# The last 448 tokens of unit 1: a short convolution on GpSimd instead of one TensorE group, with the products in one lasting tile

## The chip, the cores and the metric

The kernel runs on one core of one Trainium2 chip. The metric is the time of one execution on the device in microseconds. Three runs of the kernel before gave 765.89, 766.1 and 766.1 us; their median is 766.1.

Five engines work side by side, each in the order of its own instruction list: TensorE (PE in the profile; PEld is its loading of weights), VectorE (DVE), ScalarE (ACT), GpSimd (POOL) and SyncE (SP, used here to issue DMAs). They wait for each other through semaphores.

## What is computed

Eight sequences of 4096 tokens with 192 features pass through a causal convolution of seven taps. The features are split into eight heads of 24; each head has its own seven taps, normalised by a softmax. A feed-forward layer with a gate follows.

```python
# convolution: x (8, 4096, 192), weight (8, 7)
w = exp(weight - max) / sum                       # over the seven taps
out[b, s, h, g] = sum_k w[h, k] * x_pad[b, s + k, h, g]   # six zeros ahead of token 0
# feed-forward, on 32768 tokens, d_ff = 1536
gate = np.maximum(x @ w_gate, 0.0)
val = x @ w_val
return (gate * val @ w_out)
```

## The kernel before

**Layout.** Sequences are taken in pairs: sequence b and sequence b + 4 (called streams, st = 0 and 1). A unit is 1024 tokens of both streams, so there are 4 x 4096 / 1024 = 16 units. In the convolved input xc of a unit, the 192 features are three chunks of 64; the first 64 partitions hold stream 0, the other 64 stream 1, and tokens run along the free axis.

**A unit on TensorE.** For each window w of 512 tokens, gate_val (line 528) multiplies xc with w_gate and w_val, twelve blocks of 128 columns (line 541); ScalarE applies the Relu (line 552) and VectorE multiplies gate and value into hT (line 553). Then project (line 636) multiplies hT with w_out in eight half passes (line 570), ScalarE copies the results out of PSUM (line 596; the last of a unit is shared with VectorE) and SyncE issues their stores. So TensorE runs, unit by unit: gate_val of window 0, gate_val of window 1, project.

**The convolution of the next unit** is made beside this. GpSimd loads x with a cast to f16 (lane_load, line 203) with 64 tokens ahead of each piece (the halo), copies it into the order for the transpose (lane_turn, line 465), and SyncE issues nine DMA transposes, which give x_r with features on the partitions (line 469). The first 576 tokens of a unit (LDVE) are then made by ScalarE and VectorE: ScalarE the first tap (lane_first, line 501), VectorE the other six, three chunks each, as one multiply-and-add into acc and, for the last tap, into xc (lane_rest, line 515). VectorE has no other work in that stretch, which lies beside project. The other 448 tokens (LPOOL) are made from products per tap, written into prods by ScalarE and VectorE (line 485 and 487; the five of VectorE are listed in VECTOR, among them tap 1 of chunk 2 as the last), which GpSimd adds up in the next unit (add, line 491): six adds over 3 x 448 elements, the last one into xc. The piece of 448 tokens that is loaded and multiplied with unit v is that of unit v + 1, so that GpSimd has a whole unit for its adds.

**The start.** Unit 0 has nothing ahead of it, so both its windows are convolved on TensorE (conv_dense, line 377), with matrices (bands) that hold the taps along a diagonal. Unit 1's first 576 tokens are made as usual during unit 0. Its last 448 tokens have no unit before them to be multiplied in: they are loaded as a third group of four blocks of 112 tokens (load_x(2)), convolved by eight matmuls between unit 0's gate_val and its project (conv, line 411), cast out of PSUM by five ScalarE instructions into y (conv_out, line 430), and turned by four DMA transposes into xc of unit 1 (conv_turn, line 453).

**Order.** Nothing is rescheduled: each engine's instructions stand in the order in which the program issues them (manual_schedule), and semaphores follow from the tiles that they read and write. GpSimd's order at the start is: copies of weights to the second 64 partitions (pool_halves), w_out's load (Wo), more copies, the load of unit 1, a copy of the taps to the second 64 partitions (tap), the load of the third group, the copies of unit 1 for its transposes; then, in the loop, the load of unit 2, which is held until ScalarE's first lane_first instruction. The 448-token products of each unit take a fresh prods tile from a pool with one buffer. In unit 1 two products (FOR_POOL) are made by GpSimd.

Of the kernel before, what the change touches and what calls it, by code (L numbers as in the profile page):

```python
# [8 lines left out]
FP = mybir.dt.float32  # L9
# [6 lines left out]
def kernel(  # L16
# [38 lines left out]
    FIRST = WIN - DSUB * (GSUB - 1)  # L55
    GROUPS = [(0, [0] + [FIRST + DSUB * j for j in range(GSUB - 1)])]
    GROUPS += [(0, [WIN + DSUB * j for j in range(GSUB)])]
    GROUPS += [(0, list(range(UNIT + LDVE, 2 * UNIT, SUB)))]

    ctx.enter_context(tc.manual_schedule())  # L60
    const = ctx.enter_context(tc.tile_pool(name="const", bufs=1))
# [1 line left out]
    epool = ctx.enter_context(tc.tile_pool(name="epool", bufs=1))  # L63
    rpool = ctx.enter_context(tc.tile_pool(name="rpool", bufs=2))
    apool = ctx.enter_context(tc.tile_pool(name="apool", bufs=1))
    ypool = ctx.enter_context(tc.tile_pool(name="ypool", bufs=1))
    xcpool = ctx.enter_context(tc.tile_pool(name="xcpool", bufs=3))
    hpool = ctx.enter_context(tc.tile_pool(name="hpool", bufs=2))
    gpool = ctx.enter_context(tc.tile_pool(name="gpool", bufs=3))
# [4 lines left out]
    def load_x(g):  # L74


        bp, toks = GROUPS[g]
        n, rows, step = len(toks), SUB if g < 2 else 128, toks[1] - toks[0]
        xt = xts[g] = xpool.tile([128, GSUB, 2, D], F16, name="x_h")
        for st in range(2):  # L80
            src = bass.AP(
                tensor=x.tensor,
                offset=x.offset + ((bp + NB * st) * S + toks[0] - PAD) * D,
                ap=[[D, rows], [step * D, n], [1, D]],
            )
            nc.gpsimd.dma_start(out=xt[0:rows, 0:n, st, :], in_=src)
            yield

    def load_rest(steps):
        for _ in steps:  # L90
            pass
# [87 lines left out]
    def pool_halves(s):  # L179
        both_halves(nc.gpsimd.tensor_copy, s, Wg)  # L180
        both_halves(nc.gpsimd.tensor_copy, s, Wv)
# [160 lines left out]
    def band(h):  # L342
        return bands[h]
# [2 lines left out]

    PLACE = {0: (0, 0, 0), 1: (0, 0, 1), 3: (0, 1, 0), 4: (0, 1, 1)}
    PLACE |= {6: (1, 0, 0), 7: (1, 0, 1), 2: (1, 1, 0), 5: (1, 1, 1)}  # L350

    def conv_dense(g, c, ps, bank):


# [44 lines left out]
        conv_dense(1, 2, one, 0)  # L399
        nc.vector.tensor_copy(out=xc[0][:, 2, WIN : 2 * WIN], in_=one[:, 0, :])  # L400

    def conv(g):


        xt = xts[g]
        n = len(GROUPS[g][1])
        rows = SUB + PAD
        W = 2 * n * G
        wide = [psum.tile([128, 2, 512], FP, name="ps") for _ in range(2)]
        for h, (t, bank, slot) in PLACE.items():  # L410
            nc.tensor.matmul(  # L411
                out=wide[t][0:SUB, bank, W * slot : W * (slot + 1)],
                lhsT=band(h),
                rhs=xt[0:rows, 0:n, :, G * h : G * (h + 1)],
                start=True,
                stop=True,
                skip_group_check=True,
            )
        return wide

    def conv_out(g, wide):
        bp, toks = GROUPS[g]
        n = len(toks)
        W = 2 * n * G
        y = ypool.tile([128, GSUB, NCH, 2, 64], F16, name="y")

        def move(copy, t, bank, i0, step_in, c, r0, step_out, width):
            src = wide[t][0:SUB, bank, 0 : 2 * W]
            dst = y[0:SUB, 0:n, 0, :, 0:1]
            copy(  # L430
                out=bass.AP(
                    tensor=dst.tensor,
                    offset=dst.offset + 128 * c + r0,
                    ap=[dst.ap[0], [step_out, 2], [NCH * 128, n], [64, 2], [1, width]],
                ),
                in_=bass.AP(
                    tensor=src.tensor,
                    offset=src.offset + i0,
                    ap=[src.ap[0], [W + step_in, 2], [2 * G, n], [G, 2], [1, width]],
                ),  # L440
            )

        move(nc.scalar.copy, 0, 0, 0, 0, 0, 0, G, G)
        move(nc.scalar.copy, 0, 1, 0, 0, 1, 8, G, G)
        move(nc.scalar.copy, 1, 0, 0, 0, 2, 16, G, G)
        move(nc.scalar.copy, 1, 1, 0, 8, 0, 48, 2 * 128 - 48, 16)
        move(nc.scalar.copy, 1, 1, 16, -16, 1, 0, 56, 8)
        return y

    def conv_turn(g, y):  # L450
        for jj, t in enumerate(GROUPS[g][1]):
            u, k = t // UNIT, min(SUB, UNIT - t % UNIT)
            nc.sync.dma_start_transpose(
                out=xc[u][:, :, t % UNIT : t % UNIT + k],
                in_=y[0:k, jj].rearrange("p c s r -> p (c s r)"),
            )

    def lane_turn(v):
        xe = xes.pop(v)
        xp = epool.tile([128, TILES, NCH, 2, 64], F16, name="x_p")  # L460
        xr = rpool.tile([128, NCH, 128 * TILES], F16, name="x_r")
        xrs[v] = xr
        for j0, n, _ in pieces(v):
            for st in range(2):
                nc.gpsimd.tensor_copy(  # L465
                    out=xp[:, j0 : j0 + n, :, st, :], in_=xe[:, j0 : j0 + n, st, :, :]
                )
            for j in range(j0, j0 + n):
                nc.sync.dma_start_transpose(
                    out=xr[:, :, 128 * j : 128 * j + 128],  # L470
                    in_=xp[:, j].rearrange("p c s r -> p (c s r)"),
                )
            yield

    def shifted(v, c, k, lane):
        o = HALO - KW + 1 + k
# [34 lines left out]
    def lane_rest(v):  # L511
        acc = accs.pop(v)
        for k in range(1, KW):
            for c in range(NCH):
                nc.vector.scalar_tensor_tensor(  # L515
                    out=xc[v][:, c, 0:LDVE] if k == KW - 1 else acc[:, c, :],
                    in0=shifted(v, c, k, 0),
                    scalar=tap[:, c, k : k + 1],
                    in1=acc[:, c, :],
                    op0=ALU.mult,  # L520
                    op1=ALU.add,
                )
        if v + 1 < NUNIT:
            prods[v] = apool.tile([128, KW, NCH, LPOOL], FP, name="prods")
            for c, k in VECTOR:
                product(nc.vector, v, c, k)

# [108 lines left out]
    def project(u, hs, work):  # L636
        bp, w0 = u * UNIT // S, u * UNIT % S // WIN
        at, done = {}, {}
        order = [(0, 0), (1, 0), (0, 1), (2, 0), (1, 1), (3, 0), (2, 1), (3, 1)]
        if u == NUNIT - 1:  # L640
            order = [(0, 0), (1, 0), (0, 1), (1, 1), (2, 2), (3, 2)]
        for i, turn in order:
            h, st = hs[i // 2], i % 2
            row0 = (bp + NB * st) * S + WIN * (w0 + i // 2)
            if turn == 2:
                whole_half(h, st, row0, i == 3)
                continue
            if turn == 0:
                at[i] = slots()
            else:  # L650
                for c, k in work[i]:
                    product(nc.scalar, u + 1, c, k)
            done[i] = half_pass(h, st, at[i][1], turn, done.get(i))
            if turn:
                evict(at[i][0], row0, i == 3)
# [3 lines left out]
    both_halves(nc.vector.tensor_copy, 1, Wg)  # L659
    both_halves(nc.vector.tensor_copy, 1, Wv)  # L660
    pool_halves(4)
    nc.gpsimd.dma_start(out=Wo[:], in_=moe_w_out.rearrange("(c p) d -> p c d", p=128))
    pool_halves(5)
    load_rest(lane_load(1))
    nc.gpsimd.tensor_copy(out=tap[64:128], in_=tap[0:64])
    load_rest(load_x(2))
    load_rest(lane_turn(1))
    for u in range(NUNIT):
        adds = 1 <= u < NUNIT - 1
        if u + 1 < NUNIT:  # L670
            xc[u + 1] = xcpool.tile([128, NCH, UNIT], F16, name="xc")
        if adds:
            add(u, 1)
        hs = []
        if u == 0:
            hs.append(gate_val(0, 0))
        if 0 < u < NUNIT - 1:
            load_rest(lane_turn(u + 1))
        if 0 < u < NUNIT - 2:
            load_rest(lane_load(u + 2))  # L680
        if u == 1:
            for c, k in FOR_POOL:
                product(nc.gpsimd, u, c, k)
        if adds:
            for k in range(2, KW):
                add(u, k)
        while len(hs) < 2:
            hs.append(gate_val(u, len(hs)))
        del xc[u]
        work = [[] for _ in range(4)]  # L690
        wide = conv(2) if u == 0 else None
        if u + 1 < NUNIT:
            begun = lane_first(u + 1)
            if u == 0:
                y = conv_out(2, wide)
                load_rest(lane_load(2, begun))
            lane_rest(u + 1)
        if u + 2 < NUNIT:
            todo = [(c, k) for k in (0, 1, 2, 3, 4, 6) for c in range(NCH)]
            todo = [ck for ck in todo if ck not in VECTOR + (FOR_POOL if u == 0 else [])]  # L700
            work = [todo[a:b] for a, b in zip([0, 5, 10, 15], [5, 10, 15, 16])]
        project(u, hs, work)
        if u == 0:
            conv_turn(2, y)


# [28 lines left out]
```

## Time and profile before

| | |
|---|---|
| median of three runs | 766.1 us |
| span of the profiled execution | 764.4 us |
| TensorE busy | 760.3 us (99%) |
| VectorE busy | 705.6 us (92%) |
| ScalarE busy | 600.9 us (79%) |
| GpSimd busy | 378.4 us (50%) |
| granted TensorE clock | 1.000 |

The profile is one execution, and the span goes from its first instruction to its last. In the views below, a row of the timeline is: start in us, length in us, engine, line, operation, what it writes and reads, its shape, and how many instructions are merged in it; in brackets the idle time ahead of it and what ended that. The chain is the sequence of work that ended last, followed back from the last instruction.

### The profile page before, as it was taken

The numbers are of one execution on the slowest core, as the hardware profiler recorded it, in microseconds if no ns is written. First come the engines' busy times: TensorE is split into PE (matmuls) and PEld (weight loads), VectorE is DVE, ScalarE is ACT, GpSimd is POOL, SyncE is SP. The second block draws the span as 40 slices with busy tenths as digits, with TensorE's granted clock in tenths as the row PEclk, the third lists the DMA queues.
The fourth block names the chain that finished last, engine by engine and source line by source line (L and its number), as shares of the span: only waits on it lengthen the run. The fifth ranks groups of instructions, "written<-read, shape, count | busy, mean of one in ns | idle before, by whom it ended". The sixth has DMA issues, their size and how long they took to land.

```text
span 764.4 us, 25103 instructions
## 1 busy us (share of the span) xinstructions
PE 760.3 (99%) x10929; PEld 501.3 (66%) x10929; DVE 705.6 (92%) x763; ACT 600.9 (79%) x735; POOL 378.4 (50%) x244
## 2 busy tenths in 40 slices
PE   9999999999999999999999999999999999999998
PEld 5494674947649476584855848567494674947648
DVE  7998999999999999999999999999999999999891
ACT  6787887878878887887878878787787887876571
POOL 9419448093571926729175390853909347090000
PEclk9999999999999999999999999999999999999999
DMA  9969039290452805528073271722819134220202
GB/s 123 134 102 148 7 96 81 65 111 22 95 67 83 97 23 107 49 85 94 30 112 40 85 94 44 120 16 90 89 44 125 13 97 60 66 48 15 71 1 84
DMA packets 131830, 56.00 MB, mean 73 GB/s; under 512 B 96392, under 2 KB 131720, under 8 KB 131720
## 3 DMA queue, kind: packets, MB, share of 16 engines
q1 hardware_dynamic: 90680, 38.81, 23.9%
q0 software_dynamic: 40896, 15.50, 20.3%
q8 instruction: 85, 1.39, 0.8%
q14 instruction: 25, 0.20, 0.1%
q10 hardware_dynamic: 144, 0.10, 0.0%
HBM read 31.48 MB, written 25.17 MB: 74 GB/s over the span
## 4 chain that ended last, share of the span: by engine, by line
PE 99%; DVE 0%; ACT 0%; issue 0%
PE ps L541 65%; PE ps L570 32%; PE ps L619 1%; PE ps L377 0%; PE ps L154 0%; PE ps L411 0%; DVE band L329 0%; PE ps L272 0%; ACT acc L596 0%; PE ps L292 0%
## 5 line engine op out<-in xcount | busy, mean ns | idle before, releaser
L553 DVE TENSOR_TENSOR hT<-gr,ps 128x1024 f16<-128x1024 f16 (+1 forms) x386 | 469.0, 1216 | 36.6 <-ACT gr L552 9.4
L552 ACT ACTIVATE gr<-ps 128x1024 f16<-128x1024 f32 (+1 forms) x386 | 392.9, 1019 | 101.9 <-PE ps L541 99.7
L491 POOL TENSOR_TENSOR prods<-prods 128x1344 f32<-128x1344 f32 x70 | 212.4, 3034 | 290.0 <-DVE prods L487 286.7
L541 PE MATMUL ps<-xc,Wg 64*128 64x512 f16 x2304 | 311.9, 376 | 0.0
L541 PE MATMUL ps<-xc,Wv 64*128 64x512 f16 x2304 | 311.9, 376 | 0.0
L570 PEld LDWEIGHTS <-hT 64*128 64x128 f16 x5952 | 245.9, 94 | 3.7
L570 PE MATMUL ps<-Wo,hT 64*128 64x192 f16 x5952 | 248.1, 243 | 0.0
L541 PEld LDWEIGHTS <-Wv 64*128 64x128 f16 x2304 | 129.8, 94 | 118.5 <-DVE hT L553 0.3
L541 PEld LDWEIGHTS <-Wg 64*128 64x128 f16 x2304 | 112.3, 94 | 132.8 <-issue 0.2
L515 DVE SCALAR_TENSOR_TENSOR acc<-x_r,tap,acc 128x576 f32<-128x576 f16 x225 | 165.3, 813 | 0.0
L485 ACT ACTIVATE prods<-x_r,tap 128x448 f32<-128x448 f16 x222 | 130.1, 660 | 0.0
L596 ACT COPY out_s<-ps 128x768 f32<-128x768 f32 (+1 forms) x64 | 45.5, 711 | 51.3 <-PE ps L570 40.0
L203 POOL DMA_DIRECT2D x_e<-in_x_dram x58 | 47.0, 823 | 16.6 <-ACT acc L501 12.8
L465 POOL COPY x_p<-x_e 128x960 f16<-128x960 f16 (+1 forms) x58 | 50.3, 906 | 1.2 <-DMA x_e<-in_x_dram 1.1
L491 POOL TENSOR_TENSOR xc<-prods 128x1344 f16<-128x1344 f32 x14 | 42.4, 3029 | 1.1
L515 DVE SCALAR_TENSOR_TENSOR xc<-x_r,tap,acc 128x576 f16<-128x576 f16 x45 | 34.1, 813 | 0.0
L501 ACT ACTIVATE acc<-x_r,tap 128x576 f32<-128x576 f16 x45 | 31.4, 763 | 0.0
L487 DVE TENSOR_SCALAR prods<-x_r,tap 128x448 f32<-128x448 f16 x70 | 26.6, 450 | 0.0
L596 DVE COPY out_s<-ps 128x384 f32<-128x384 f32 (+1 forms) x16 | 8.7, 541 | 11.9 <-PE ps L619 9.4
L619 PE MATMUL ps<-Wo,hT 128*128 128x192 f16 x96 | 8.1, 246 | 0.0
L619 PEld LDWEIGHTS <-hT 128*128 128x128 f16 x96 | 7.9, 98 | 0.2 <-issue 0.2
L154 PE MATMUL ps<-const-bfloat16-1.0 128*128 128x512 bf16 (+1 forms) x9 | 3.9, 572 | 0.8 <-PEq L719 0.8
(54 smaller groups left out, 56.3 us busy)
## 6 DMA issues: line engine op xcount, KB each, us to landing
out_dram<-out_s SPq DMA_DIRECT2D x62, 384.0 KB, 2.7
x_e<-in_x_dram POOLq DMA_DIRECT2D x34, 192.0 KB, 7.4
x_e<-in_x_dram POOLq DMA_DIRECT2D x24, 240.0 KB, 5.6
x_r<-x_p SPq DMA_TRANSPOSE x131, 5.1
Wo<-in_moe_w_out_dram POOLq DMA_DIRECT2D x1, 576.0 KB, 7.3
x_h<-in_x_dram POOLq DMA_DIRECT2D x2, 210.0 KB, 4.8
Wg<-in_moe_w_gate_dram POOLq DMA_DIRECT2D x4, 96.0 KB, 4.1
Wv<-in_moe_w_val_dram POOLq DMA_DIRECT2D x4, 96.0 KB, 4.0
```

The source lines that it names most:

```text
L203: first = nc.gpsimd.dma_start(out=xe[:, j0 + start : j0 + n, st, :, :].rearrange("p j c r -> p j (c r)"), in_=bass.AP(tensor=x.tensor, off ...
L465: nc.gpsimd.tensor_copy(out=xp[:, j0 : j0 + n, :, st, :], in_=xe[:, j0 : j0 + n, st, :, :])
L485: engine.activation(out=out, in_=in_, func=ACTF.Copy, scale=scale)
L487: engine.tensor_scalar(out=out, in0=in_, scalar1=scale, scalar2=None, op0=ALU.mult)
L491: nc.gpsimd.tensor_tensor(out=pr[:, 0] if k < KW - 1 else xc[v + 1][:, :, LDVE:UNIT], in0=pr[:, 0], in1=pr[:, k], op=ALU.add,)
L501: nc.scalar.activation(out=accs[v][:, c, :], in_=shifted(v, c, 0, 0), func=ACTF.Copy, scale=tap[:, c, 0:1],)
L515: nc.vector.scalar_tensor_tensor(out=xc[v][:, c, 0:LDVE] if k == KW - 1 else acc[:, c, :], in0=shifted(v, c, k, 0), scalar=tap[:, c, k : k ...
L541: nc.tensor.matmul(out=pss[i][:, st, :], lhsT=W[64 * st : 64 * st + 64, c, 128 * f : 128 * (f + 1)], rhs=xcb[64 * st : 64 * st + 64, c, WI ...
L552: nc.scalar.activation(out=gr[:, sts], in_=pss[0][:, sts], func=ACTF.Relu)
L553: nc.vector.tensor_tensor(out=h[:, f, sts], in0=gr[:, sts], in1=pss[1][:, sts], op=ALU.mult)
L570: mm = nc.tensor.matmul(out=outs[q], lhsT=h[64 * r : 64 * r + 64, f, st, 128 * q : 128 * (q + 1)], rhs=Wo[64 * r : 64 * r + 64, f, :], sta ...
L596: one(out=dst[:, step * j : step * j + step], in_=src[:, step * j : step * j + step])
```

## The change

The eight matmuls, the five casts and the four transposes of the third group go, with their load and their pool. GpSimd convolves these 448 tokens instead: for each tap a product of 128 x 3 x 448 elements, in which the tap is read with a step of zero along the tokens, and an add of it to a running sum. The product of the last tap is made by ScalarE, as three activations ahead of the second eviction of unit 0. The input comes from a load of its own (four blocks of 128 tokens, the halo among them), two GpSimd copies and four DMA transposes, issued ahead of unit 1's nine.

GpSimd's order becomes: the new load, the last copies of weights, the first two loads of unit 1, the two copies for the new transposes, the other loads of unit 1, its first copies, the tap copy, the load of Wo, the other copies, then the first four of the twelve steps, unit 2's load, seven more steps, and the last add. Unit 2's copies follow, then unit 1's usual adds; unit 3's load moves behind these. The products of all units share one tile (room, which also serves as a staging place at the start), and ScalarE makes the products of tap 0 last instead of first.

```diff
-    GROUPS += [(0, list(range(UNIT + LDVE, 2 * UNIT, SUB)))]
...
-    ypool = ctx.enter_context(tc.tile_pool(name="ypool", bufs=1))
+    spool = ctx.enter_context(tc.tile_pool(name="spool", bufs=1))
...
+    SIDE = (LPOOL + HALO) // 128
+    side = {}
+
+    def side_load():
+        xe = side["x"] = xpool.tile([128, GSUB, 2, D], F16, name="x_h")
+        for st in range(2):
+            nc.gpsimd.dma_start(
+                out=xe[:, 0:SIDE, st, :],
+                in_=bass.AP(
+                    tensor=x.tensor,
+                    offset=x.offset + (NB * st * S + UNIT + LDVE - HALO) * D,
+                    ap=[[D, 128], [128 * D, SIDE], [1, D]],
+                ),
+            )
+
+    def side_turn():
+        xe = side.pop("x")
+        xp = xpool.tile([128, GSUB, 2, D], F16, name="x_h")
...
+        side["r"] = spool.tile([128, NCH, 128 * SIDE], F16, name="side_r")
+        for st in range(2):
+            nc.gpsimd.tensor_copy(
+                out=xp[:, :, :, st, :],
+                in_=xe[:, 0:SIDE, st, :].rearrange("p j (c r) -> p j c r", r=64),
+            )
+        for j in range(SIDE):
+            nc.sync.dma_start_transpose(
+                out=side["r"][:, :, 128 * j : 128 * j + 128],
+                in_=xp[:, j].rearrange("p c s r -> p (c s r)"),
+            )
+        for name in ("acc", "one", "last"):
+            side[name] = spool.tile([128, NCH, LPOOL], FP, name=f"side_{name}")
+
+    def side_in(k):
+        o = HALO - KW + 1 + k
+        return side["r"][:, :, o : o + LPOOL]
+
+    def side_steps(lo, hi):
+        steps = [(0, 0)] + [(k, what) for k in range(1, KW) for what in range(k == KW - 1, 2)]
+        for k, what in steps[lo:hi]:
+            one = side["last" if k == KW - 1 else "one"]
+            if what == 0:
+                nc.gpsimd.tensor_tensor(
+                    out=side["acc"][:] if k == 0 else one[:],
+                    in0=side_in(k),
+                    in1=tap[:, :, k : k + 1].to_broadcast([128, NCH, LPOOL]),
+                    op=ALU.mult,
+                )
+                continue
+            nc.gpsimd.tensor_tensor(
+                out=xc[1][:, :, LDVE:UNIT] if k == KW - 1 else side["acc"][:],
+                in0=side["acc"][:],
+                in1=one[:],
+                op=ALU.add,
+            )
...
-            prods[v] = apool.tile([128, KW, NCH, LPOOL], FP, name="prods")
+            prods[v] = room
...
+                if u == 0 and i == 1:
+                    for c in range(NCH):
+                        nc.scalar.activation(
+                            out=side["last"][:, c, :],
+                            in_=side_in(KW - 1)[:, c, :],
+                            func=ACTF.Copy,
+                            scale=tap[:, c, KW - 1 : KW],
+                        )
+                    side_steps(11, 12)
...
     pool_halves(4)
+    side_load()
+    pool_halves(5)
+    first_lane = lane_load(1)
+    next(first_lane)
+    next(first_lane)
+    side_turn()
+    load_rest(first_lane)
+    turns = lane_turn(1)
+    next(turns)
+    nc.gpsimd.tensor_copy(out=tap[64:128], in_=tap[0:64])
     nc.gpsimd.dma_start(out=Wo[:], in_=moe_w_out.rearrange("(c p) d -> p c d", p=128))
-    pool_halves(5)
-    load_rest(lane_load(1))
-    nc.gpsimd.tensor_copy(out=tap[64:128], in_=tap[0:64])
-    load_rest(load_x(2))
-    load_rest(lane_turn(1))
+    load_rest(turns)
+    side_steps(0, 4)
...
-        if adds:
+        if adds and u > 1:
             add(u, 1)
...
-        if 0 < u < NUNIT - 2:
+        if 1 < u < NUNIT - 2:
             load_rest(lane_load(u + 2))
         if u == 1:
+            add(u, 1)
             for c, k in FOR_POOL:
                 product(nc.gpsimd, u, c, k)
         if adds:
             for k in range(2, KW):
                 add(u, k)
+        if u == 1:
+            load_rest(lane_load(u + 2))
...
-        wide = conv(2) if u == 0 else None
...
-                y = conv_out(2, wide)
                 load_rest(lane_load(2, begun))
+                side_steps(4, 11)
...
-            todo = [(c, k) for k in (0, 1, 2, 3, 4, 6) for c in range(NCH)]
+            todo = [(c, k) for k in (1, 2, 3, 4, 6, 0) for c in range(NCH)]
...
-        if u == 0:
-            conv_turn(2, y)
```

More of the change, by code (lines that the diff above doesn't have):

```diff
@@ L77, in load_x @@
         bp, toks = GROUPS[g]
-        n, rows, step = len(toks), SUB if g < 2 else 128, toks[1] - toks[0]
+        n, rows, step = len(toks), SUB, toks[1] - toks[0]
         xt = xts[g] = xpool.tile([128, GSUB, 2, D], F16, name="x_h")
@@ L345 @@
     xc = {}
-    PLACE = {0: (0, 0, 0), 1: (0, 0, 1), 3: (0, 1, 0), 4: (0, 1, 1)}
-    PLACE |= {6: (1, 0, 0), 7: (1, 0, 1), 2: (1, 1, 0), 5: (1, 1, 1)}
     def conv_dense(g, c, ps, bank):
@@ L400, in second_block @@
         nc.vector.tensor_copy(out=xc[0][:, 2, WIN : 2 * WIN], in_=one[:, 0, :])
[L402 to L456, printed above, removed]
     def lane_turn(v):
@@ L473, in lane_turn @@
             yield
+    SIDE = (LPOOL + HALO) // 128
[14 more added lines that the diff above has]
+        xp = xpool.tile([128, GSUB, 2, D], F16, name="x_h")
+        xp = xp[:, 0:SIDE].rearrange("p j s d -> p j (s d)").rearrange("p j (c s r) -> p j c s r", s=2, r=64)
+        side["r"] = spool.tile([128, NCH, 128 * SIDE], F16, name="side_r")
[32 more added lines that the diff above has]
+            )
     def shifted(v, c, k, lane):
```

## The prediction

> **What bounds the kernel now.** I read the page's busy times first, then its chain of work that ended last, then that chain in order of time, then the timelines of VectorE, GpSimd and ScalarE around unit 0's projection.
>
> ```profile
> span 764.4 us, 25103 instructions
> PE 760.3 (99%) x10929; PEld 501.3 (66%) x10929; DVE 705.6 (92%) x763; ACT 600.9 (79%) x735; POOL 378.4 (50%) x244
> PE 99%; DVE 0%; ACT 0%; issue 0%
> PE ps L541 65%; PE ps L570 32%; PE ps L619 1%; PE ps L377 0%; PE ps L154 0%; PE ps L411 0%; DVE band L329 0%; PE ps L272 0%; ACT acc L596 0%; PE ps L292 0%
> ```
>
> TensorE sets the time: it is busy 760.3 of 764.4 us and is 99% of the chain. So the change can save only what it takes off TensorE, and every wait that it puts in front of TensorE is paid in full. The chain in order of time (start, length, what) shows how much can come off:
>
> ```profile
> 40.60 0.91 PE ps L411 x8
> 41.51 15.95 PE ps L570 x384
> 57.46 31.08 PE ps L541 x288
> 88.54 15.84 PE ps L570 x384
> 104.38 31.08 PE ps L541 x288
> ```
>
> L411 is the group that goes: 0.91 us. Unit 0's projection takes 15.95 where every later unit takes 15.84, so 0.11 more may go with it, 1.02 in all. That is 0.13% of 766.1; a measurement of this kernel can tell about 0.2%, 1.5 us, from no change. A visible gain is nearly excluded, and the question is what the added work does to TensorE's two next inputs: unit 1's first window (tokens 0 to 511, all from VectorE) and its second (tokens 576 to 1023 from the changed part).
>
> With 1.02 gone, TensorE asks for the first window at 57.46 - 1.02 = 56.44, and for the second half of 31.08 later, 56.44 + 15.54 = 71.98.
>
> VectorE's timeline (start, length, what):
>
> ```profile
> 17.71 24.55 DVE L553 TENSOR_TENSOR hT<-gr,ps 128x1024 f16<-128x1024 f16 x19 [1.06 <-ACT gr L552]
> 42.18 11.02 DVE L515 SCALAR_TENSOR_TENSOR acc<-x_r,tap,acc 128x576 f32<-128x576 f16 x15
> 53.12 2.27 DVE L515 SCALAR_TENSOR_TENSOR xc<-x_r,tap,acc 128x576 f16<-128x576 f16 x3
> 55.30 1.90 DVE L487 TENSOR_SCALAR prods<-x_r,tap 128x448 f32<-128x448 f16 x5
> 59.20 31.01 DVE L553 TENSOR_TENSOR hT<-gr,ps 128x1024 f16<-128x1024 f16 x24 [0.59 <-ACT gr L552]
> ```
>
> The first window is ready at 53.12 + 2.27 = 55.39: after the change only 1.05 us ahead of its use. VectorE has no gap from 42.18 to there, 13.21 us of L515.
>
> **The change part by part.** *Taken away.* The eight matmuls (-1.02, above). ScalarE's five casts to y and SP's four transposes of y:
>
> ```profile
> 42.90 1.66 ACT L430 CAST y<-ps 112x384 f16<-112x384 f32 x5
> 44.42 2.94 ACT L485 ACTIVATE prods<-x_r,tap 128x448 f32<-128x448 f16 x5
> 51.56 0.80 ACT L596 COPY out_s<-ps 128x768 f32<-128x768 f32 x1 [0.36 <-PE ps L570]
> ```
>
> ScalarE gets back three activations of 448, at 2.94/5 = 0.59 each 1.76 us, for the casts' 1.66. They stand ahead of the eviction that was at 51.56; it slides by under 1.5 us, covered by ScalarE's waits for TensorE around it and by the three later evictions' buffers. I cost it at 0; without that cover it would be 1.5.
>
> *GpSimd's chain.* Twelve instructions over 128x1344 now make tokens 576 to 1023: six products (a tap broadcast along 448 tokens), six adds, each waiting for the one before, and four DMA issues between the fourth and the fifth. GpSimd's rows:
>
> ```profile
> 16.62 1.05 POOL L662 DMA_DIRECT2D Wo<-in_moe_w_out_dram  x1
> 17.67 1.16 POOL L177 COPY Wg<-Wg 64x1152 f16<-64x1152 f16 x1
> 19.84 3.23 POOL L203 DMA_DIRECT2D x_e<-in_x_dram  x4
> 23.17 1.51 POOL L86 DMA_DIRECT2D x_h<-in_x_dram  x2
> 26.60 1.83 POOL L465 COPY x_p<-x_e 128x960 f16<-128x960 f16 x2 [0.22 <-DMA x_e<-in_x_dram]
> 28.64 0.83 POOL L465 COPY x_p<-x_e 128x768 f16<-128x768 f16 x1 [0.21 <-DMA x_e<-in_x_dram]
> 42.22 3.19 POOL L203 DMA_DIRECT2D x_e<-in_x_dram  x4 [12.75 <-ACT acc L501]
> 67.34 2.83 POOL L487 TENSOR_SCALAR prods<-x_r,tap 128x448 f32<-128x448 f16 x2
> 70.12 12.36 POOL L491 TENSOR_TENSOR prods<-prods 128x1344 f32<-128x1344 f32 x4
> 82.56 3.03 POOL L491 TENSOR_TENSOR xc<-prods 128x1344 f16<-128x1344 f32 x1
> ```
>
> Until 16.62 nothing moves. Then: two issues of the new x_h load 1.51 (18.1), two copies of Wg and Wv 2.2 (20.3), two issues of x_e 1.6 (21.9). The new load lands 4.8 us (below) behind its second issue at 17.4, at 22.2. Two copies of 768 elements, 1.7 (23.9); two issues 1.6 (25.5); two copies of 960, 1.9 (27.4); the tap copy and Wo's issue 1.2 (28.6); then two copies of 768, whose data were issued by 25.5 and land by 31 (31.3).
>
> The queue's side of it:
>
> ```profile
> x_h<-in_x_dram POOLq DMA_DIRECT2D x2, 210.0 KB, 4.8
> Wo<-in_moe_w_out_dram POOLq DMA_DIRECT2D x1, 576.0 KB, 7.3
> 27.61 12.39 SPq L469 DMA_TRANSPOSE x_r<-x_p  x9
> ```
>
> SP issues a transpose every 12.39/9 = 1.38 us, so the four new ones stand from 23.9 to 29.4 and have landed at about 31. Unit 1's nine follow, the first five (that ScalarE and VectorE need at 41 to 42) issued by 29.4 + 6.9 = 36.3: covered, with some 2 us of landing to spare for each side. Wo moves behind the lane loads: issued by 28.6, landed by 36, for a first use at 40.6; cost 0, and 4.6 us of cover.
>
> So the first product starts at about 31.5. The adds' own row gives the price of a link of the chain: four in 12.36, of which the last takes 3.03 as the one at 82.56 does, thus (12.36 - 3.03)/3 = 3.11. The product is not in the trace. Its bounds: GpSimd's own products of 448 tokens take 2.83/2, for three times the tokens 4.3; copies of 768 elements 0.83, at that rate 1.4. I take 3.11, since it has two tensor inputs as the add has. Then: four links to 31.5 + 12.4 = 43.9, four issues to 47.1, seven links to 68.9, the last add to 72.0. The need is at 71.98. The chain just meets it if nothing slows it, and has no reserve.
>
> *What it runs beside.* From 42.18 on this chain runs beside L515. In the kernel before that pair never meets, as GpSimd's waits and its busy time in three L515 stretches (the second number of a window's row, after its length) show:
>
> ```profile
> POOL prods L491 <- DVE prods L487: 286.7, 14, 22.9
> core 0: us, POOL busy (x), PEclk, DMA share, GB/s
> 42.18:55.39 13.21, 3.19 (x4) 1.00 0.81 130
> 89.50:103.30 13.80, 0.00 (x0) 1.00 0.19 59
> 136.50:150.00 13.50, 0.00 (x0) 1.00 0.19 61
> ```
>
> The 3.19 is DMA issuing. So the price of the meeting is unknown, and its bounds are nothing and full exclusion (only one of the two at a time). For nothing speak the adds at 67 to 85, which run beside L553 at no visible cost: 31.01/24 = 1.29 each there, and 24.55/19 = 1.29 from 17.71 on, where GpSimd has no adds; but L553 has one input in PSUM, L515 two in SBUF. For exclusion speak two equal copies of VectorE, both beside GpSimd's DMA issuing, of which one took twice as long:
>
> ```profile
> 6.49 0.28 DVE L177 COPY Wg<-Wg 64x384 f16<-64x384 f16 x1 [0.27 <-DMA Wg<-in_moe_w_gate_dram]
> 6.75 0.58 DVE L177 COPY Wv<-Wv 64x384 f16<-64x384 f16 x1
> 6.44 1.63 POOL L86 DMA_DIRECT2D x_h<-in_x_dram  x2
> ```
>
> So these two engines can hold each other up. I take exclusion, with VectorE in front: its L515 follow every 11.02/15 = 0.735 us (the row above) with no gap, while GpSimd's links leave 0.08 between them.
>
> The Trainium skill, "SBUF — State Buffer", section "Who interferes with whom", says that a VectorE instruction with two SBUF inputs contends with a GpSimd instruction that reads SBUF, and that the later of the two waits for the whole of the other. The pair of copies agrees that they can block; no run here shows it for L515. By that rule the time is my forecast's or rival 2's, without it rival 1's.
>
> *The sum.* The chain's fourth link (40.8 to 43.9) holds L515 back by 1.7; L515 ends at 43.9 + 13.21 = 57.1, 0.7 after the need. GpSimd's remaining eight links then start at 57.1 and end at 57.1 + 8 x 3.11 = 82.0; TensorE asks for the second window at 57.1 + 15.54 = 72.6 and waits 9.4. In unit 1 GpSimd's usual adds, pushed from 85 to about 107, meet the next L515 and cost 0.6 more. Together -1.0 + 0.7 + 9.4 + 0.6 = +9.7 on the profile's 764.4; the runs' median lies 1.7 above that span, so 766.1 + 9.7, about **775.5**. If the last eight links slip in partly, or products are cheaper, it comes down to 769; if L487 excludes as well, 777.5.
>
> *The rest* I cost at 0: the lasting product tile and ScalarE's order with tap 0 last let unit 2's products follow unit 1's later adds tap by tap; the last add of unit 1 (107) is due at 119.9 + 9. Later units keep their order.
>
> **Rivals.** *1, not slower: no exclusion, products at the adds' price.* The chain ends at 72.0, TensorE waits 0 to 2 and has saved 1.02: 765.1 to 767. For it: L553 beside the adds. Against: no reserve, and two SBUF inputs on both sides.
>
> *2, they take turns, one L515 per link.* VectorE does five during the issues, then one per 3.03 + 0.74 = 3.77; eight links from 47.6 end at 77, with L515 12 done, and the six left, between GpSimd's next copies, at 85. TensorE waits for the first window from 56.4 to 85: +28.6 - 1.0, about 793. For it: a waiting engine would get its turn; it would explain best why the two are kept apart. Against: L515's gapless order.
>
> *3, no exclusion, products at GpSimd's 448-token price.* Six links dearer by 1.2 to 1.3 end the chain at 79.6; wait 7.6, net +6.6: 772.7. Against: that is another operation. The Trainium skill, "GPSIMD Engine Reference", section "Elementwise — side-by-side cycle accounting", puts an instruction with two tensor inputs at 2.6 cycles an element; by it the product would be an add, an estimate of 2.9 us (1344 x 2.6 / 1.2 GHz). The adds' 3.03 agrees.
>
> **How the numbers follow.** Forecast 0.35, rival 1 0.30, rival 2 0.21, rival 3 0.12, and 0.02 that more than L411 comes off. Slower by over 0.2%: 0.35 + 0.21 + 0.12 = 0.68; within: 0.30; faster: 0.02. The forecast's own range is 769 to 778. The wide one takes in rival 1 from its best (764.8) and half of rival 2 (to 790).
>
> **What would show it.** Right: L411 gone and L570 following at once; GpSimd's remaining links stretched or pushed behind L515; a gap of TensorE before unit 1's second window, released by GpSimd's last add into xc. Rival 1: that gap under 2 us, L515 still 0.81 each. Rival 2: L515 several us apart, the gap before the first window. Rival 3: L515 untouched, products over 4 us. What would make it wrong: a chain that starts well before 31.5, x_r or Wo landing after 41, or products well under 3 us.

## The result and the profile after

| | before | after |
|---|---|---|
| median of five runs | 765.89 us (765.73 to 766.1) | 793.76 us (792.3 to 794.16) |
| span of the profiled execution | 764.4 us | 790.6 us |

The ratio is 1.0359, with a 95% interval of 1.0347 to 1.0372. The change makes the kernel 27.9 us slower.

The page of the changed kernel first: its busy times and its chain.

```profile
span 790.6 us, 25070 instructions
PE 762.2 (96%) x10921; PEld 521.9 (66%) x10921; DVE 731.8 (93%) x763; ACT 601.0 (76%) x733; POOL 417.7 (53%) x258
PE 94%; DVE 5%; issue 0%; ACT 0%; DVEq 0%
PE ps L539 63%; PE ps L568 29%; DVE acc L513 5%; PE ps L617 1%; PE ps L153 0%; PE ps L373 0%; DVE xc L513 0%; ACT gr L550 0%; PE ps L291 0%; PE ps L271 0%; ACT acc L594 0%; DVEq L513 0%; DVEq L485 0%; DVE hT L551 0%; DVEq L594 0%
```

VectorE had 0% of the chain of before, none of it on L515, and now has 5%, nearly all on L513. That is L515 of before, the multiply-and-adds of a unit's first 576 tokens. Other lines have moved likewise: gate_val is L539 here, project L568, VectorE's products L485, the usual adds L489, unit loads L202 and their copies L405. The new GpSimd products are L459 and the new adds L466. In the runs below the same L513 stands up to three lines further down. The chain in order of time shows where VectorE comes in (some of its pieces):

```profile
16.23 24.11 PE ps L539 x222
42.56 37.79 DVE acc L513 x15
82.59 32.15 PE ps L539 x284
114.74 15.84 PE ps L568 x384
```

The fifteen L513 into acc took 11.02 us before and 37.79 now. TensorE's own timeline gives what that cost it (in brackets the idle time ahead and what ended it):

```profile
40.80 16.04 PE L568 MATMUL ps<-Wo,hT 64*128 64x192 f16 x384
81.14 2.07 PE L539 MATMUL ps<-xc,Wg 64*128 64x512 f16 x6 [24.30 <-DVE xc L513]
```

Unit 0's projection follows gate_val at once and ends at 56.84; TensorE then waits 24.30 us for unit 1's first window, which VectorE makes. It is not the window whose convolution was moved.

GpSimd's timeline beside that stretch (the four steps from 56.60 on, left out here, go on in the same way):

```profile
33.35 2.43 POOL L459 TENSOR_TENSOR side_acc<-side_r,tap 128x1344 f32<-128x1344 f16 x1 [1.54 <-DMA side_r<-x_h]
38.25 3.04 POOL L466 TENSOR_TENSOR side_acc<-side_acc,side_one 128x1344 f32<-128x1344 f32 x1
41.37 2.44 POOL L459 TENSOR_TENSOR side_one<-side_r,tap 128x1344 f32<-128x1344 f16 x1
43.74 3.28 POOL L202 DMA_DIRECT2D x_e<-in_x_dram  x4
47.03 3.05 POOL L466 TENSOR_TENSOR side_acc<-side_acc,side_one 128x1344 f32<-128x1344 f32 x1
50.17 2.83 POOL L459 TENSOR_TENSOR side_one<-side_r,tap 128x1344 f32<-128x1344 f16 x1
53.08 3.44 POOL L466 TENSOR_TENSOR side_acc<-side_acc,side_one 128x1344 f32<-128x1344 f32 x1
69.37 3.41 POOL L466 TENSOR_TENSOR xc<-side_acc,side_last 128x1344 f16<-128x1344 f32 x1
72.72 5.56 POOL L405 COPY x_p<-x_e 128x960 f16<-128x960 f16 x4
```

and VectorE's, one instruction a row (a selection; the last row has GpSimd idle beside it):

```profile
42.56 1.85 DVE L513 SCALAR_TENSOR_TENSOR acc<-x_r,tap,acc 128x576 f32<-128x576 f16 x1
44.34 6.37 DVE L513 SCALAR_TENSOR_TENSOR acc<-x_r,tap,acc 128x576 f32<-128x576 f16 x1
50.63 2.98 DVE L513 SCALAR_TENSOR_TENSOR acc<-x_r,tap,acc 128x576 f32<-128x576 f16 x1
53.54 3.59 DVE L513 SCALAR_TENSOR_TENSOR acc<-x_r,tap,acc 128x576 f32<-128x576 f16 x1
69.83 3.56 DVE L513 SCALAR_TENSOR_TENSOR acc<-x_r,tap,acc 128x576 f32<-128x576 f16 x1
78.82 0.81 DVE L513 SCALAR_TENSOR_TENSOR acc<-x_r,tap,acc 128x576 f32<-128x576 f16 x1
```

Read them side by side. An L513 takes 2.98 beside a product of 2.83 and 3.59 beside an add of 3.44; alone it takes 0.81. Each ends about 0.6 us after the GpSimd step beside it. By then GpSimd's next step has begun, and the next L513 lasts to 0.6 us after the end of that one. For every step of GpSimd one L513 gets through, until the steps and the four copies behind them are over. (The second L513, 6.37 us, lasted through GpSimd's DMA issues as well; more on this below.) GpSimd pays too, but less: an add takes 3.4 instead of 3.04, a product 2.83 instead of 2.43. The last add is done at 72.78, well ahead of its use, 15.5 us behind 81.14.

A second loss is in the granted clock. The rows show stretches of time, each with the busy times of PE, PEld, DVE, ACT and POOL, then the clock, which was 1.00 before:

```profile
58.00:62.00 4.00, 0.00 (x0) 0.00 (x0) 4.00 (x2) 0.00 (x0) 3.92 (x2) 0.93 0.30 98
62.00:70.00 8.00, 0.00 (x0) 0.00 (x0) 8.00 (x4) 0.00 (x0) 7.76 (x4) 0.50 0.00 0
81.00:83.00 2.00, 1.62 (x8) 0.39 (x9) 2.00 (x5) 0.00 (x0) 0.00 (x0) 0.50 0.00 0
83.00:85.00 2.00, 2.00 (x12) 0.86 (x10) 2.00 (x6) 1.02 (x1) 0.50 (x1) 0.50 0.00 0
85.00:86.00 1.00, 1.00 (x10) 0.51 (x8) 0.95 (x1) 0.36 (x1) 1.00 (x1) 0.85 0.22 71
86.00:90.00 4.00, 4.00 (x42) 2.08 (x38) 3.16 (x3) 3.19 (x4) 4.00 (x3) 1.00 0.67 157
```

While TensorE idles its clock falls to half, and stays there for the first 4.2 us of work, from 81.14 to about 85.3. The Trainium skill, "TensorE: Matmul & The Clock Gate", Part 1, says that the clock goes to half after an idle window of about 3.4 us and returns after as long a busy one; the trace agrees, with half by 62 after an end at 56.84, and full again between 85 and 86. In the paused run below less was enough: a gap of 2.74 and two of 0.34 close together, and the clock was 0.57 from 120 to 122.

Unit 1's gate_val lasts from 81.14 to 114.74, 33.60 instead of 31.08, which is 2.52 more. Of this the clock explains about 2.1 at most, an estimate: 4.2 us at half the clock are 2.1 us of work undone. The rest are short waits. The window's second and third chunk come from VectorE 0.73 us apart behind the first, and TensorE is busy for 1.62 us of the 1.86 between its start at 81.14 and 83.

The account of the span: from the second block to the end of unit 0's projection 41.60 before (15.86 to 57.46), 40.61 after (16.23 to 56.84), so -0.99; a start that was 0.37 later; the gap +24.30; the slower gate_val behind it +2.52. Together +26.2, which is 790.6 - 764.4. The profiled run is the fastest of the five, 792.3; the median is 1.5 above it.

### The profile page after: what moved, and what is told of

It is laid out like the page before. It is cut to its first block, busy times and chain, and to the rows that moved or that the text cites. A ratio compares the mean times of both kernels' runs of the same rounds, so it can differ in the third digit from the quotient of the medians.

```text
span 790.6 us, 25070 instructions
## 1 busy us (share of the span) xinstructions
PE 762.2 (96%) x10921; PEld 521.9 (66%) x10921; DVE 731.8 (93%) x763; ACT 601.0 (76%) x733; POOL 417.7 (53%) x258
## 4 chain that ended last, share of the span: by engine, by line
PE 94%; DVE 5%; issue 0%; ACT 0%; DVEq 0%
PE ps L539 63%; PE ps L568 29%; DVE acc L513 5%; PE ps L617 1%; PE ps L153 0%; PE ps L373 0%; DVE xc L513 0%; ACT gr L550 0%; PE ps L291 0%; PE ps L271 0%; ACT acc L594 0%; DVEq L513 0%; DVEq L485 0%; DVE hT L551 0%; DVEq L594 0%
## 5 line engine op out<-in xcount | busy, mean ns | idle before, releaser
L489 POOL TENSOR_TENSOR prods<-prods 128x1344 f32<-128x1344 f32 x70 | 212.3, 3033 | 287.1 <-DVE prods L485 283.7
L539 PE MATMUL ps<-xc,Wg 64*128 64x512 f16 x2304 | 317.9, 377 | 24.5 <-DVE xc L513 24.3
L539 PE MATMUL ps<-xc,Wv 64*128 64x512 f16 x2304 | 317.0, 377 | 0.0
L568 PEld LDWEIGHTS <-hT 64*128 64x128 f16 x5952 | 246.3, 94 | 3.5
L568 PE MATMUL ps<-Wo,hT 64*128 64x192 f16 x5952 | 248.4, 243 | 0.0
L539 PEld LDWEIGHTS <-Wg 64*128 64x128 f16 x2304 | 125.7, 94 | 145.6 <-DVE xc L513 24.5
L539 PEld LDWEIGHTS <-Wv 64*128 64x128 f16 x2304 | 137.0, 94 | 112.1 <-issue 1.0
L513 DVE SCALAR_TENSOR_TENSOR acc<-x_r,tap,acc 128x576 f32<-128x576 f16 x225 | 192.1, 931 | 0.0
L405 POOL COPY x_p<-x_e 128x960 f16<-128x960 f16 (+1 forms) x58 | 52.6, 948 | 1.3 <-DMA x_e<-in_x_dram 1.2
L202 POOL DMA_DIRECT2D x_e<-in_x_dram x58 | 47.1, 820 | 3.5 <-POOL x_p L405 2.4
L489 POOL TENSOR_TENSOR xc<-prods 128x1344 f16<-128x1344 f32 x14 | 42.4, 3027 | 1.1
L513 DVE SCALAR_TENSOR_TENSOR xc<-x_r,tap,acc 128x576 f16<-128x576 f16 x45 | 34.0, 811 | 0.0
L485 DVE TENSOR_SCALAR prods<-x_r,tap 128x448 f32<-128x448 f16 x70 | 26.6, 446 | 0.0
L466 POOL TENSOR_TENSOR side_acc<-side_acc,side_one 128x1344 f32<-128x1344 f32 x5 | 16.3, 3266 | 0.3
L459 POOL TENSOR_TENSOR side_one<-side_r,tap 128x1344 f32<-128x1344 f16 x5 | 13.4, 2670 | 0.3
## 6 DMA issues: line engine op xcount, KB each, us to landing
Wo<-in_moe_w_out_dram POOLq DMA_DIRECT2D x1, 576.0 KB, 10.2
```

What stands on the lines that cost most here:

```text
L202: first = nc.gpsimd.dma_start(out=xe[:, j0 + start : j0 + n, st, :, :].rearrange("p j c r -> p j (c r)"), in_=bass.AP(tensor=x.tensor, off ...
L405: nc.gpsimd.tensor_copy(out=xp[:, j0 : j0 + n, :, st, :], in_=xe[:, j0 : j0 + n, st, :, :])
L485: engine.tensor_scalar(out=out, in0=in_, scalar1=scale, scalar2=None, op0=ALU.mult)
L489: nc.gpsimd.tensor_tensor(out=pr[:, 0] if k < KW - 1 else xc[v + 1][:, :, LDVE:UNIT], in0=pr[:, 0], in1=pr[:, k], op=ALU.add,)
L513: nc.vector.scalar_tensor_tensor(out=xc[v][:, c, 0:LDVE] if k == KW - 1 else acc[:, c, :], in0=shifted(v, c, k, 0), scalar=tap[:, c, k : k ...
L539: nc.tensor.matmul(out=pss[i][:, st, :], lhsT=W[64 * st : 64 * st + 64, c, 128 * f : 128 * (f + 1)], rhs=xcb[64 * st : 64 * st + 64, c, WI ...
```

## The experiments

Each was run beside the kernel before, at 765.99 to 766.07 us. Where one time is given it is one execution, and its profile. The marks "run 1" and "run 2" in the cuts of code are put in here.

**Without the middle steps.**

```diff
-                side_steps(4, 11)
```

> Leaves out GpSimd's seven steps between unit 2's load and the last add (four adds and three products); all else is the changed kernel. Turn theory (VectorE's L513 and GpSimd's steps take turns, one instruction each): L513 back at one every 0.735 us, held only about 1 us by the fourth step; no gap of TensorE over 0.5 us; time 0.3 to 1.0 us under the kernel before, ratio 0.9987 to 0.9997. Rival (another part of the change, such as the order of loads or the lasting tile, costs time): still over 770 us.

Measured: 766.69, ratio 1.0009, interval 1.0000 to 1.0017. This kernel leaves out that part of unit 1's convolution. L513 is at its own pace again and the gap is gone: all but 0.1% of the loss comes from these seven steps beside L513.

```profile
43.97 11.14 DVE L513 SCALAR_TENSOR_TENSOR acc<-x_r,tap,acc 128x576 f32<-128x576 f16 x15
```

The expected gain did not appear. In its profile unit 0's projection followed gate_val at once (42.38 to 58.55, 16.17 instead of 16.86 with the group), but the second stretch of unit 0 began at 17.64 instead of 15.86. This start was anywhere from 15.71 to 17.64 in the profiles of the changed kernels, and the twelve runs reach from 765.27 to 769.62; what moves it stays open.

One row of it matters below, from GpSimd's timeline: the last add came at 53.72, beside a running L513, and was held until VectorE's L513 and the five L485 behind them were over.

```profile
53.72 8.28 POOL L466 TENSOR_TENSOR xc<-side_acc,side_last 128x1344 f16<-128x1344 f32 x1 [6.20 <-ACT side_last L653]
```

**Two parts alone**, in the kernel before: the lasting tile, and ScalarE's tap 0 last.

```diff
-            prods[v] = apool.tile([128, KW, NCH, LPOOL], FP, name="prods")
+            prods[v] = room
...
-            todo = [(c, k) for k in (0, 1, 2, 3, 4, 6) for c in range(NCH)]
+            todo = [(c, k) for k in (1, 2, 3, 4, 6, 0) for c in range(NCH)]
```

> The kernel before with two parts of the change alone: the lasting tile for the products, and ScalarE's products of tap 0 last. All theories: the same as before, ratio 0.999 to 1.001, L515 at 0.735 apart; any other outcome would put a part of the loss on them.

Measured: 766.06, ratio 1.0003 (0.9995 to 1.0012). These parts cost nothing.

**Which GpSimd work excludes L513?** Memsets, and copies with one input, in place of the seven steps, so that part of the convolution is left out here too:

```diff
-                side_steps(4, 11)
+                for _ in range(14):
+                    nc.gpsimd.memset(side["one"][:], 0.0)   # run 1
+                    nc.gpsimd.tensor_copy(out=side["one"][:], in_=side["acc"][:])   # run 2
```

> The seven steps are replaced by fourteen memsets of 128x1344, which read nothing from SBUF (that part of unit 1's convolution is left out). If only GpSimd's reads exclude L513: L513 at 0.735 us apart, time about 765. If any GpSimd work on SBUF does: each L513 waits for a memset of about 1.2 us, 14 turns, TensorE waits about 8 us or more, 774 to 778.

> GpSimd's seven steps after unit 2's load replaced by fourteen f32 copies of 128x1344, one input from SBUF each (that part of the convolution is left out). If any GpSimd instruction that reads SBUF excludes L513: L513 at about 1.9 us per turn, 14 turns, TensorE's gap about 15 us, 779 to 784 us. If it takes two inputs on both sides: L513 at 0.81, 765 to 767.

Measured: 774.07 with memsets, 790.05 with copies. VectorE's timeline beside the memsets (the first L513 waited for the fourth step):

```profile
42.69 13.01 DVE L513 SCALAR_TENSOR_TENSOR acc<-x_r,tap,acc 128x576 f32<-128x576 f16 x15
57.82 6.32 DVE L485 TENSOR_SCALAR prods<-x_r,tap 128x448 f32<-128x448 f16 x5
```

and one L513 beside the copies:

```profile
59.57 1.85 DVE L513 SCALAR_TENSOR_TENSOR acc<-x_r,tap,acc 128x576 f32<-128x576 f16 x1
```

Beside memsets L513 runs at its own pace; beside copies it takes turns as expected (14 copies, 24.89 us). So what excludes L513 is a GpSimd instruction that reads SBUF, be it one input or two. The memset run took 8 us more than the kernel before because another pair met: L485, VectorE's product from one SBUF input, took 1.90 for five before and 6.32 here, and TensorE then waited 5.0 us for VectorE's share of an eviction behind it, with a lower clock after that. In the copies run L485 was held too, by the last of the copies, the last add and unit 2's copies behind it (7.7 us for five). TensorE waited 4.94 us for it, which is most of the 6 us by which that run lies above the expected range. The Trainium skill, "SBUF — State Buffer", section "Who interferes with whom", says that a VectorE instruction with two SBUF inputs contends with a GpSimd instruction that reads SBUF and not with one that only writes it, while a tensor_scalar, which can run in a two-port mode, contends with GpSimd in that mode without this exception. These runs agree for L513 and L485 beside memsets and beside copies; that L485 ran in that mode is not shown by itself.

**The pair by itself**, in the kernel before, far from the change: six spare adds beside the last L515 stretch, released ahead of it, by the fifth L515, or by ScalarE's first eviction. Two theories stand against each other: strict turns, and a lead, by which the engine that is already running back to back keeps the other out. The cut shows the helper; the three runs differ in what they hand it as hold.

```diff
+    def spare_adds(v, hold):
+        pr = prods[v]
+        for _ in range(6):
+            made = nc.gpsimd.tensor_tensor(out=pr[:, 0], in0=pr[:, 0], in1=pr[:, 1], op=ALU.add)
+            if hold is not None:
+                tc.add_manual_dep(made.ins, hold.ins.name, SYNC, reason="spare adds")
+                hold = None
```

> The kernel before, with six spare GpSimd adds (as in line 491, over old data, result unused) beside the last L515 stretch, at 700 us, that start with ScalarE's first L501, ahead of VectorE's first L515. Turn theory with GpSimd in the lead: six L515 at 3 to 3.6 us, 6 x 2.76 = 16.5 us more, of which about 1.5 are hidden; with 1 to 2 us at a lower clock 781 to 784 us. Rival (something particular to the start of the kernel, not the pair): L515 at 0.81, time as before.

> The same six spare adds, but the first waits for the fifth L515. Lead theory: L515 untouched at 0.81, the first add held until the last L515, time as before within 0.3%. Strict turns: as in the run with the adds first, 778 to 783 us.

> The kernel before with the six spare adds beside the last L515 stretch, released by ScalarE's first eviction of that projection instead of by an L515. In the run without the middle steps one add that ScalarE had released was held for 5.2 us behind L513 and L485; in the runs with adds released by VectorE turns began at once. If the releasing engine makes the difference: the first add is held until the last L515 and time stays within 0.3% of before. If not: six turns of 3.5 us, 781 to 785 us, and the held add stays unexplained.

Measured: 783.14, 783.35 and 765.89. The first shows that the pair alone does it, far from the start of the kernel: six L515 at 3.3 to 3.6 and a TensorE gap of 13.84. The second refutes the lead theory as a rule: VectorE ran back to back, and the first add still got in at once. GpSimd's row and one of VectorE's:

```profile
704.19 3.47 POOL L534 TENSOR_TENSOR prods<-prods 128x1344 f32<-128x1344 f32 x1 [15.31 <-DVE acc L515]
```

```profile
708.20 3.58 DVE L515 SCALAR_TENSOR_TENSOR acc<-x_r,tap,acc 128x576 f32<-128x576 f16 x1
```

In the third the same add was kept out until the last L515, and TensorE lost nothing. Its rows of GpSimd and VectorE:

```profile
705.25 10.77 POOL L531 TENSOR_TENSOR prods<-prods 128x1344 f32<-128x1344 f32 x1 [16.74 <-ACT out_s L604]
```

```profile
704.29 6.65 DVE L515 SCALAR_TENSOR_TENSOR acc<-x_r,tap,acc 128x576 f32<-128x576 f16 x9
710.86 2.27 DVE L515 SCALAR_TENSOR_TENSOR xc<-x_r,tap,acc 128x576 f16<-128x576 f16 x3
```

**The same question in the changed kernel**: the fifth step held, by one of VectorE's L513 or by ScalarE's first eviction.

```diff
-                side_steps(4, 11)
...
+            if u == 0:
+                side_steps(4, 11, end)   # run 1, behind lane_rest; end is its fifth L513
...
+                if u == 0 and i == 0:
+                    side_steps(4, 11, made)   # run 2, behind evict
```

> The changed kernel, but the fifth GpSimd step waits for the sixth of unit 1's eighteen L513 (tap 2, chunk 1, is the fifth), so that it comes while VectorE is running back to back. Lead theory (whichever engine is running back to back when the other comes keeps the lead; GpSimd in the lead lets one L513 through per step, VectorE in the lead lets no step through until its two-input and product instructions are over): L513 stays at 0.81 us, the fifth step ends only about 3 us after the last L485 at 60, the rest as in the paused kernel: 780 to 785 us. Strict turns whoever leads: L513 at 3 to 3.6 us again from the sixth on, eight turns, TensorE's first gap about 20 us: 786 to 790.

> The changed kernel, but the fifth GpSimd step waits for ScalarE's first eviction of unit 0 (about 48 us), so that it comes while L513 runs; nothing left out. The run held at the fifth L513 gave 792.58 with turns, the run paused to the end of the stretch 782.9. If a release by ScalarE leaves VectorE in the lead, as it did with the spare adds: L513 at 0.81 after that point, the fifth step held to about 59, 780 to 785 us. If the releasing engine does not matter: turns again, 790 to 794 us.

Measured: 792.58 and 791.12, both with turns from the arrival on. But neither run is a clean test of the releasing engine, because the step did not wait for its release alone. GpSimd's rows of the first:

```profile
46.37 3.29 POOL L202 DMA_DIRECT2D x_e<-in_x_dram  x4
49.66 3.20 POOL L466 TENSOR_TENSOR side_acc<-side_acc,side_one 128x1344 f32<-128x1344 f32 x1
```

In the first run the fifth L513 was over at 49.23 and GpSimd issued DMAs until 49.66; in the second the eviction was over at 48.53 and the issues at 48.60. In both GpSimd came to the step straight from its issues, not out of an idle wait as in the runs with the spare adds.

Over all these runs, of six arrivals behind a wait or behind issues, beside L513 or L515 running back to back, four got their turn at once and two were kept out to the end of the stretch. In the two the arrival was 0.15 and 0.23 us behind the start of an L513 or L515, in the four 0.16 (copies), 0.22, 0.51 and 0.59: no order in that. The two had waited idle for ScalarE, the spare add that got in had waited idle for VectorE, and the other three came from issues. That leaves the releasing engine possible, but three idle waits do not show it. What decides stays open.

**Paused to the end of the stretch.**

```diff
-                side_steps(4, 11)
-            lane_rest(u + 1)
+            end = lane_rest(u + 1)
+            if u == 0:
+                side_steps(4, 11, end)
```

> The seven steps wait for the last L513 of unit 1 (a wait that is added, nothing left out). Turn theory: L513 undisturbed after the fourth step; the remaining steps run alone at 2.43 (product) and 3.1 (add), from about 57 to 80; TensorE waits about 7.5 us, now ahead of unit 1's second window, and a little over 1 us at a lower clock: 772 to 774 us. Rival (both engines are slowed by something that lasts, not by each other): steps still 2.8 and 3.4, L513 still slow, 780 or more.

Measured: 782.9, ratio 1.022 (1.0205 to 1.0235). As expected L513 (L516 in this kernel) is free behind the fourth step, the steps run at 2.43 and 3.03, and TensorE waits 8.57 us at the second window. Of the 9 us beyond the expected time 5.6 are a second meeting, which was not expected here: GpSimd's usual adds of unit 1 now last until 107.9 and run into unit 2's stretch. VectorE's timeline there:

```profile
101.81 16.21 DVE L516 SCALAR_TENSOR_TENSOR acc<-x_r,tap,acc 128x576 f32<-128x576 f16 x15
```

16.21 instead of 11.02; TensorE waits 2.74 and twice 0.34, and a lower clock follows, as behind the 8.57: unit 2's gate_val ends 36.52 us after unit 1's projection, where it was 30.91. The other part of the 9 us is in unit 1, about half of it waits of 1.84 in all at its first window.

**Two sizes of the turn.** Unit 2's load behind the twelve steps, and each step cut into three instructions of 448 elements:

```diff
-                load_rest(lane_load(2, begun))
                 side_steps(4, 11)
+                load_rest(lane_load(2, begun))
```

```diff
+            for c in range(NCH):
...
-                    out=side["acc"][:] if k == 0 else one[:],
-                    in0=side_in(k),
+                    out=(side["acc"] if k == 0 else one)[:, c, :],
+                    in0=side_in(k)[:, c, :],
```

> Unit 2's load is issued behind the twelve steps instead of between the fourth and the fifth; nothing left out. In the changed kernel one L513 took 6.37 us, across the four issues and the add behind them. If the issues themselves hold L513, they do so again at their new place: about 788 us. If it was the add waiting behind the issues, L513 runs freely during the issues, nine of them follow at 0.735, and TensorE's wait falls from 24 to about 18: about 785.

> The changed kernel with each of GpSimd's twelve steps cut into three instructions of 448 elements; nothing left out. Turns by instruction: each L513 waits for one short GpSimd instruction, about 1.25 to 1.5 us per turn instead of 2.9 to 3.5, VectorE's stretch ends near 69, TensorE's gap about 12 us, 778 to 782 us. If the two engines share by time and not by instruction: the stretch ends at 82 as in the changed kernel, 790 to 794.

Measured: 795.83 and 795.51, both above all that was expected. With the load at the end one L513 took 8.96 us, through the four issues, the last add and part of the copies. With short steps many turns were short (1.48 to 1.69), but then VectorE was kept out for several steps at a time:

```profile
71.12 10.73 DVE L514 SCALAR_TENSOR_TENSOR acc<-x_r,tap,acc 128x576 f32<-128x576 f16 x1
```

The thirds of a step do not wait for each other, but that alone does not explain it: in the same run three such thirds of a product (4.26 us) had taken turns with L514 one by one. Their row, and the L514 beside the last of them:

```profile
42.95 4.26 POOL L460 TENSOR_TENSOR side_one<-side_r,tap 128x448 f32<-128x448 f16 x3
46.34 1.48 DVE L514 SCALAR_TENSOR_TENSOR acc<-x_r,tap,acc 128x576 f32<-128x576 f16 x1
```

When several GpSimd instructions get through at a time stays open. So does what held L513 through DMA issues, here and in the 6.37 of the changed kernel. The traces give a hint: where it ran freely beside the same issues, GpSimd's next instruction behind them had to wait for another engine (the kernel before, the paused run, the one without the middle steps, the two with the fifth step held) or read nothing (memsets); where it was held through, a step that reads followed at once. Copies and short steps lie between, with 1.85 and then 0.81, and 1.69 each. No run tested it.

A version that beats both was not found: the most to be had is the 0.99 us above, and GpSimd's chain of some 33 us finds only about 9 us ahead of VectorE's stretch (33.35 to 42.2) and 17 between its end and the due time (55.4 to 72).

## Why the prediction was wrong

The direction was right, and the mechanism, exclusion between L515 and GpSimd's reading steps, was the one that the runs showed. The time was outside the range, by the step "I take exclusion, with VectorE in front: its L515 follow every 11.02/15 = 0.735 us (the row above) with no gap, while GpSimd's links leave 0.08 between them". In the changed kernel the two take turns. That turns a wait of 9.4 us at the second window into one of 24.3 at the first. The argument from gaps was no evidence for who wins: the same gapless order kept GpSimd's add out in two runs and let it in at once in others. Rival 2, which had 0.21 and the time 793, is what happened, and the range's upper end of 790 cut it in half.

Point by point:

- **Taken off TensorE:** 1.02 predicted, 0.99 measured.
- **Start of the chain:** 31.5 predicted, 33.35 measured; the four transposes landed later. **Price of a product:** 3.11 taken, 2.43 measured alone, so this product (f16 input, tap read with step zero) is cheaper than an add of two f32 tiles, and also under the 2.9 estimated at rival 3; which of its two inputs makes it so was not separated. The two errors cancel by luck: the fourth step ended at 43.81, against 43.9.
- **The forecast's own sum:** 766.1 + 9.7 is 775.8, not 775.5. The difference is small against the miss.
- **Rival 2's sum:** 28.6 - 1.0 on 766.1 is 793.7, given as 793. Its gap of 28.6 stands against 24.30. Its turn was sized too dear, 3.77 for each of eight; measured 25.75/8 = 3.22, since steps and L513 overlap by about 0.4 and products are shorter. It had VectorE free during the issues, where it was held.
- **Clock:** no term of the sum. With the short waits behind the gap it cost 2.52, which made good part of what the gap was sized too long; that 793 was so near was partly luck.
- **Cost 0:** the lasting tile and tap 0 last are shown to cost nothing. Wo landed 10.2 us after its issue at 28.2, still ahead of 40.8. The second meeting in unit 1 did not come in the changed kernel, where all of VectorE's work was late as well; it did in the paused one, and there cost 5.6, several times the 0.6 that was put on it.
- **Rivals 1 and 3** fall with L513 at 3 us and the product at 2.43.

## What to carry to other kernels

Ahead of moving work to an idle engine, look at what the critical engine's supplier runs in that stretch: if the idle engine has been idle there in every unit, that itself has to be explained. Here a VectorE instruction with two SBUF inputs and a GpSimd instruction that reads SBUF did not run at once, so GpSimd's "free" time was paid by VectorE: its fifteen L513 took 26.8 us longer. When exclusion is the likely mechanism, put the strict alternation inside the range: here a 0.7 us instruction beside a 3 us one became a 3 us one.

## What the hardware showed unexpectedly

Which engine yields is not fixed: the same add got in at once (3.47 us) in one run and was kept out for 7.7 us (10.77 in all) in another, with an L515 running back to back in both. L485, with one SBUF input, was held by GpSimd's memsets, 6.32 us for five against 1.90, though L513 with two was not.
